# Reading the last 4 rows per partition of the last batch of K by a four-block transfer on four DMA engines

## Chip, cores, metric

The kernel runs on one core of one Trainium2 chip. The metric is device microseconds of one execution, as a median of several executions. Before the change it was 139.41 us (three runs, 139.39 to 139.55).

## The reference, cut to what matters

The program is one decode step of a transformer block for 4 sequences: layer norm, attention over the last 2,048 cached positions (4 key/value heads of 128, 32 query heads), residual, layer norm, gated feed-forward, residual. Everything is bf16.

```python
Hkv, Sk = k_cache.shape[1], k_cache.shape[2]          # 4, 8192
W = min(4096, max(256, Sk // 4))                      # 2048
k = jnp.repeat(k_cache[:, :, Sk - W:, :], rep, axis=1)
scores = jnp.einsum("bhqd,bhkd->bhqk", q, k) * (Dh ** -0.5)
p = _softmax(scores, axis=-1)
...
h2 = h + _B_ref(_layernorm(h, axis=-1), B_w1, B_w3, B_w2)
```

One execution reads 55.6 MB: the query weights, 2 MB of keys and 2 MB of values per sequence, the output weights, and three feed-forward matrices. Each byte is used once.

## The kernel before

All large loads are issued on the SyncE queue (SP), in order, into five buffers of 32 KB per partition. The order is query weights, keys of batches 0 to 3, values of batches 0 to 3, output weights, `w1`, `w3`, `w2`. Keys of one batch go to 128 partitions, 64 rows (16 KB) to each; partition `p` holds block `p // 4` of head `p % 4`.

```python
def load_k(b):
    t = stream.tile([P, SLOT], BF16, tag="s")
    out = []
    for k in range(BS):
        v = t[:, k * JK * Dh : (k + 1) * JK * Dh]
        nc.sync.dma_start(
            out=v,
            in_=A_k_cache[b + k, :, Sk - W : Sk, :].rearrange("g (pp j) d -> pp g (j d)", pp=PK),
        )
        out.append(v)
    return out
# ... (values: four runs of 4 KB to a partition)

def emit_scores(u):
    b, n = units[u]
    kT_v = kT_tiles[u][:].rearrange("d j (pp g) -> d g j pp", g=Hkv)
    for g in range(Hkv):
        nc.tensor.matmul(
            scores_ps[QD * g : QD * (g + 1), n * 512 : (n + 1) * 512],
            lhsT=qz[:, b, g * QD : (g + 1) * QD],
            rhs=kT_v[:, g, :, :], start=(b == 0), stop=(b == B - 1),
        )
# ... (softmax, values, output projection, feed-forward)
# the last load, w2, comes in pieces of 16, 5, 4, 2 and 1 rows per partition
```

## Time and profile before

| | before |
|---|---|
| median time | 139.41 us |
| span of the profiled run | 137.4 us |
| mean rate of the loads | 406 GB/s |
| last of 16 completions of the last load | 133.59 us |

These are the busy times, the rows of the 40 time slices, and the queues, from the page of the kernel before. Each digit of the DMA row is the busy tenth of the 16 DMA engines in a slice; the row below it is what they moved.

```profile
span 137.4 us, 2307 instructions
...
PE 71.2 (52%) x1045; PEld 45.2 (33%) x1045; DVE 36.3 (26%) x63; ACT 29.0 (21%) x28; POOL 1.6 (1%) x7
...
PE   0152304798989889100995579544090530802960
...
DMA  5999999999999999999999999999999999998950
GB/s 155 444 402 520 391 391 444 420 429 444 405 440 392 421 421 414 423 495 476 401 391 424 453 428 397 459 467 401 409 459 439 426 409 430 448 458 359 420 217 2
DMA packets 4773, 55.74 MB, mean 406 GB/s; under 512 B 376, under 2 KB 408, under 8 KB 2716
...
q1 hardware_dynamic: 4724, 55.58, 95.4%
q8 instruction: 8, 0.13, 0.3%
...
q14 instruction: 1, 0.01, 0.0%
```

PE (the matmuls; PEld is the loading of their weights) is busy 52% of the span and no other compute engine more than 26%, and the DMA row is full from the second slice to the end of the loads: the kernel is bound by its stream of loads. The lines q8 and q14 are small. They are DMA packets of the kind that the profile calls "instruction"; the records below show them taking turns with the data packets on the same 16 DMA engines.

The end of the chain of waits of the kernel before (start us, length us, what) says which load that is. The line below it is from the time line.

```profile
95.17 37.81 DMA t<-in_B_w_dram
132.98 0.04 issue
133.02 1.04 PE y_ps L428 x9
134.06 0.02 issue
134.09 0.42 DVE res L438
```

```profile
133.64 0.11 PEld L428 LDWEIGHTS <-hgT 128*32 128x32 bf16 x3 [0.30 <-issue]
```

The matmuls wait for the last piece of the weights but one until 132.98 us. The last piece lands at 133.59 us (below), and the last four matmuls start just after, at about 133.64 us; the chain calls this last gap "issue" and does not name the load. A copy and the store follow.

The second reading needs the engines one by one. The trace has 16 completion writes for each large load and four for each of the small loads of `x`, which have 4 rows (6.50, 6.56, 6.61 and 6.72 us for one of them). They are read here as one by each engine that takes part. The kernel before:

```
load                        its 16 completions, us
keys, batch 3               41.54 to 42.07 (14 engines)   43.27  43.45
values, batch 0             46.51 to 47.02 (14)           48.17  48.19
w1, first half              89.29 to 89.77 (9)   90.63   90.89 to 91.10 (6)
w2, last piece              131.79 to 132.28 (7)   133.00   133.34 to 133.59 (8)
instruction packets         16 KB at 31.70 41.45 52.82 72.20 78.17 83.90 104.06 130.81, 8 KB at 81.93
```

The engines start nearly level (7.52 to 8.16 us for the first large load, 12.42 to 12.91 for the second) and fall apart one by one. The packet records show why. Each 16 KB instruction packet takes 0.88 to 0.96 us and begins where a data packet of one engine ends, and that engine is 1.40 to 1.42 us behind for the rest of the run; no two of the eight fall on the same engine. The single 8 KB packet sets one engine back by 0.84 us. The last of the 16 engines ends the stream of loads, so 7 engines idle for more than a microsecond at the end.

For later comparison, two microseconds of the stretch table of the kernel before (the busy time of each engine in a stretch of the span, with the number of its instructions), in the load of the first values. The last two columns are the DMA engines' busy share and GB/s (a share above 1 is possible, since a packet counts whole in the microsecond in which it starts, and neighbours overlap by a few ns: the 4 KB packets take 159 ns each and follow at about 155).

```profile
core 0: us, PE busy (x) PEld busy (x) DVE busy (x) ACT busy (x) POOL busy (x), PEclk, DMA share, GB/s
...
42.00:43.00 1.00, 1.00 (x21) 1.00 (x20) 0.43 (x1) 0.00 (x0) 0.00 (x0) 1.00 0.97 389
43.00:44.00 1.00, 0.87 (x16) 0.79 (x14) 0.80 (x2) 1.00 (x2) 0.00 (x0) 1.00 1.03 426
```

### The profile page before, as it was taken

The numbers are of one execution on the slowest core, as the hardware profiler recorded it, in microseconds if no ns is written. First come the engines' busy times: TensorE is split into PE (matmuls) and PEld (weight loads), VectorE is DVE, ScalarE is ACT, GpSimd is POOL, SyncE is SP. The second block draws the span as 40 slices with busy tenths as digits, with TensorE's granted clock in tenths as the row PEclk, the third lists the DMA queues.
The fourth block names the chain that finished last, engine by engine and source line by source line (L and its number), as shares of the span: only waits on it lengthen the run. The fifth ranks groups of instructions, "written<-read, shape, count | busy, mean of one in ns | idle before, by whom it ended". The sixth has DMA issues, their size and how long they took to land.

```text
span 137.4 us, 2307 instructions
## 1 busy us (share of the span) xinstructions
PE 71.2 (52%) x1045; PEld 45.2 (33%) x1045; DVE 36.3 (26%) x63; ACT 29.0 (21%) x28; POOL 1.6 (1%) x7
## 2 busy tenths in 40 slices
PE   0152304798989889100995579544090530802960
PEld 0110001175656565000894457221030210302830
DVE  6430000244444444601400300530003970160001
ACT  0400000155564646098610000000005000000000
POOL 4000000000000000000000000000000000000000
PEclk9999999999999999975555555558655586555555
DMA  5999999999999999999999999999999999998950
GB/s 155 444 402 520 391 391 444 420 429 444 405 440 392 421 421 414 423 495 476 401 391 424 453 428 397 459 467 401 409 459 439 426 409 430 448 458 359 420 217 2
DMA packets 4773, 55.74 MB, mean 406 GB/s; under 512 B 376, under 2 KB 408, under 8 KB 2716
## 3 DMA queue, kind: packets, MB, share of 16 engines
q1 hardware_dynamic: 4724, 55.58, 95.4%
q8 instruction: 8, 0.13, 0.3%
q10 hardware_dynamic: 40, 0.02, 0.0%
q14 instruction: 1, 0.01, 0.0%
HBM read 55.59 MB, written 0.01 MB: 405 GB/s over the span
## 4 chain that ended last, share of the span: by engine, by line
DMA 70%; PE 19%; ACT 6%; SPq 1%; DVE 1%; issue 1%; ACTq 0%
DMA t<-in_B_w_dram 54%; DMA t<-in_A_wq_dram 15%; PE kt_ps L270 9%; ACT kT L276 5%; PE scores_ps L255 5%; PE q_ps L222 3%; PE g_ps L398 2%; SPq L97 1%; PE y_ps L428 1%; DVE q_sb L232 1%; ACT q_sb L233 0%; DVE res L438 0%; PE qt_ps L236 0%; ACTq L276 0%
## 5 line engine op out<-in xcount | busy, mean ns | idle before, releaser
L276 ACT COPY kT<-kt_ps 128x1024 bf16<-128x1024 bf16 x16 | 15.8, 1014 | 12.0 <-PE kt_ps L270 12.0
L270 PE MATMUL kt_ps<-ident,t 128*128 128x128 bf16 x256 | 16.5, 219 | 0.0
L270 PEld LDWEIGHTS <-t 128*128 128x128 bf16 x256 | 14.4, 98 | 5.0 <-issue 4.9
L274 DVE COPY kT<-kt_ps 128x1024 bf16<-128x1024 bf16 x16 | 11.1, 692 | 15.2 <-PE kt_ps L270 15.2
L398 PEld LDWEIGHTS <-hnT 128*32 128x32 bf16 x128 | 5.5, 140 | 25.0 <-issue 22.7
L222 PE MATMUL q_ps<-t,xnT 128*4 128x512 bf16 x64 | 7.2, 615 | 12.0 <-DMA t<-in_A_wq_dram 12.0
L398 PE MATMUL u_ps<-t,hnT 128*32 128x448 bf16 x64 | 6.4, 576 | 10.6 <-DMA t<-in_B_w_dram 10.6
L255 PE MATMUL scores_ps<-kT,qz 128*32 128x512 bf16 x64 | 9.9, 609 | 3.1 <-ACT kT L276 3.1
L428 PE MATMUL y_ps<-t,hgT 128*32 128x256 bf16 x112 | 6.7, 415 | 7.6 <-DMA t<-in_B_w_dram 7.6
L398 PE MATMUL g_ps<-t,hnT 128*32 128x448 bf16 x64 | 6.3, 574 | 8.0 <-DMA t<-in_B_w_dram 8.0
L322 PE MATMUL OT_ps<-PT_sb,t 128*128 128x8 bf16 x256 | 7.4, 168 | 1.9 <-issue 1.7
L428 PEld LDWEIGHTS <-hgT 128*32 128x32 bf16 x112 | 4.8, 139 | 10.0 <-issue 5.5
L349 PE MATMUL y_ps<-t,o 128*32 128x256 bf16 x128 | 7.2, 418 | 1.7 <-DMA t<-in_A_wo_dram 0.9
L322 PEld LDWEIGHTS <-t 128*128 128x128 bf16 x256 | 7.3, 104 | 2.1 <-issue 2.0
L222 PEld LDWEIGHTS <-xnT 128*4 128x4 bf16 x64 | 2.0, 111 | 16.4 <-issue 16.1
L308 PE MATMUL pt_ps<-Dm,Pm 128*128 128x128 bf16 x16 | 1.9, 308 | 9.3 <-DVE Dm L301 9.3
L349 PEld LDWEIGHTS <-o 128*32 128x32 bf16 x128 | 5.1, 144 | 3.5 <-issue 1.2
L412 DVE RECIPROCAL eg<-eg 128x896 f32<-128x896 f32 x1 | 5.8, 5754 | 0.0
L232 DVE TENSOR_SCALAR q_sb<-q_ps 128x512 bf16<-128x512 f32 x1 | 0.7, 692 | 17.8 <-PE q_ps L222 17.8
L233 ACT ACTIVATE q_sb<-q_ps 128x512 bf16<-128x512 f32 x1 | 0.6, 597 | 21.4 <-DVE q_sb L232 21.4
L308 PEld LDWEIGHTS <-Pm 128*128 128x128 bf16 x16 | 1.6, 142 | 9.8 <-ACT Pm L294 9.8
L294 ACT ACTIVATE Pm<-scores_ps,nmax 128x2048 bf16<-128x2048 f32 x1 | 4.8, 4783 | 0.0
(67 smaller groups left out, 37.0 us busy)
## 6 DMA issues: line engine op xcount, KB each, us to landing
t<-in_B_w_dram SPq DMA_DIRECT2D x4, 3584.0 KB
t<-in_A_k_cache_dram SPq DMA_DIRECT2D x4, 2048.0 KB, 25.6
t<-in_A_v_cache_dram SPq DMA_DIRECT2D x4, 2048.0 KB, 33.0
t<-in_A_wo_dram SPq DMA_DIRECT2D x2, 4096.0 KB, 32.5
t<-in_A_wq_dram SPq DMA_DIRECT2D x2, 2048.0 KB, 9.6
t<-in_A_wq_dram SPq DMA_DIRECT2D x1, 4096.0 KB, 21.0
t<-in_B_w_dram SPq DMA_DIRECT2D x1, 4096.0 KB, 39.9
t<-in_B_w_dram SPq DMA_DIRECT2D x1, 1280.0 KB, 34.9
```

What stands on the lines that cost most here:

```text
L222: nc.tensor.matmul(q_ps[QD * g : QD * g + B, hf * 512 : (hf + 1) * 512], lhsT=xnT[:, kc, :], rhs=wq_t[:, c0 : c0 + 512], start=(kc == 0), ...
L255: nc.tensor.matmul(scores_ps[QD * g : QD * (g + 1), n * 512 : (n + 1) * 512], lhsT=qz[:, b, g * QD : (g + 1) * QD], rhs=kT_v[:, g, :, :], ...
L270: nc.tensor.transpose(out=kt_ps[:, jj, :], in_=k_v[:, n * NJ + t * TB + jj, :], identity=ident[:])
L274: nc.vector.tensor_copy(out=kT[:, t * TB : (t + 1) * TB, :], in_=kt_ps[:])
L276: nc.scalar.copy(out=kT[:, t * TB : (t + 1) * TB, :], in_=kt_ps[:])
L294: nc.scalar.activation(out=Pm[:].rearrange("q (c jq) -> q jq c", jq=NSB), in_=scores_ps[:].rearrange("q (jq c) -> q jq c", jq=NSB), func=A ...
L308: nc.tensor.matmul(pt_ps[:, jj, :], lhsT=Pm[:, (jb * JPB + jj) * P : (jb * JPB + jj + 1) * P], rhs=Dm[:], start=True, stop=True)
L322: nc.tensor.matmul(OT_ps[:, b, g * REP : (g + 1) * REP], lhsT=v_t[:, g, j, :], rhs=PT_sb[:, j, g * QD + b * REP : g * QD + (b + 1) * REP], ...
L349: nc.tensor.matmul(y_ps[QD * j : QD * (j + 1), :], lhsT=o4[:, i, :, :].rearrange("p b s -> p (b s)"), rhs=loaded["wo"][i][:, j * CG : (j + ...
L398: nc.tensor.matmul(out_ps[QD * j : QD * (j + 1), hf, :HF], lhsT=hnT[:, k, :], rhs=loaded[kind][k][:, c0 : c0 + HF], start=(k == 0), stop=( ...
L412: nc.vector.reciprocal(out=eg[:], in_=eg[:])
L428: nc.tensor.matmul(y2_ps[QD * j : QD * (j + 1), :], lhsT=hgT[:, i, :], rhs=loaded["w2"][i][:, j * CG : (j + 1) * CG], start=False, stop=(i ...
```

## The change

The keys of the last batch come in two transfers. The first takes 60 of 64 rows per partition, as before. The second takes the last 4 rows (1 KB per partition, 128 KB in all) with the head as the outer dimension, so as four blocks of 32 partitions. The intent: the four blocks go to four DMA engines, as the 4-row loads of `x` with their four completions let expect, so twelve engines carry 8 KB less each and four carry 24 KB more. If the four are engines that finish early, the late ones finish earlier. The last group of score matmuls is split to follow the new partition order of these rows.

```diff
+    JT = 4
...
             v = t[:, k * JK * Dh : (k + 1) * JK * Dh]
-            nc.sync.dma_start(
-                out=v,
-                in_=A_k_cache[b + k, :, Sk - W : Sk, :].rearrange("g (pp j) d -> pp g (j d)", pp=PK),
-            )
+            n = (JK - JT) * Dh if b + k == B - 1 else JK * Dh
+            k_v = A_k_cache[b + k, :, Sk - W : Sk, :].rearrange("g (pp j) d -> pp g (j d)", pp=PK)
+            nc.sync.dma_start(out=v[:, :n], in_=k_v[:, :, :n])
+            if n < JK * Dh:
+                nc.sync.dma_start(out=v[:, n:], in_=k_v.rearrange("pp g x -> g pp x")[:, :, n:])
...
+        js = NJ - JT if u == len(units) - 1 else NJ
+        for j0, j1 in ((0, js), (js, NJ)):
+            ...
+            kT_v = kT_tiles[u][:, j0:j1, :].rearrange(
+                "d j (pp g) -> d g j pp" if j0 == 0 else "d j (g pp) -> d g j pp", g=Hkv
+            )
+            # then the four matmuls, on columns n*512 + j0*PK to n*512 + j1*PK
```

More of the change, by code (lines that the diff above doesn't have):

```diff
@@ L42 @@
     KC = D // P
-    FC = F // P
     NK = W // P
     NSB = W // 512
-    assert B == 4 and D == KC * P and F == FC * P and Hq * Dh == 4096
+    assert B == 4 and D == KC * P and F % P == 0 and Hq * Dh == 4096
     assert Dh == P and W == NK * P and B * Hq == P and Hkv == 4
@@ L251, in emit_scores @@
         b, n = units[u]
-        kT_v = kT_tiles[u][:].rearrange("d j (pp g) -> d g j pp", g=Hkv)
-        for g in range(Hkv):
-            z0 = (b * Hkv + g) * QD
-            nc.tensor.matmul(
-                scores_ps[QD * g : QD * (g + 1), n * 512 : (n + 1) * 512],
-                lhsT=qz[:, b, g * QD : (g + 1) * QD],
-                rhs=kT_v[:, g, :, :],
-                start=(b == 0),
-                stop=(b == B - 1),
-            )
+        js = NJ - JT if u == len(units) - 1 else NJ
+        for j0, j1 in ((0, js), (js, NJ)):
+            if j0 == j1:
+                continue
+            kT_v = kT_tiles[u][:, j0:j1, :].rearrange(
+                "d j (pp g) -> d g j pp" if j0 == 0 else "d j (g pp) -> d g j pp", g=Hkv
+            )
+            for g in range(Hkv):
+                nc.tensor.matmul(
+                    scores_ps[QD * g : QD * (g + 1), n * 512 + j0 * PK : n * 512 + j1 * PK],
+                    lhsT=qz[:, b, g * QD : (g + 1) * QD],
+                    rhs=kT_v[:, g, :, :],
+                    start=(b == 0),
+                    stop=(b == B - 1),
+                    skip_group_check=True,
+                )
     nt = 0
```

## The prediction

> What bounds the kernel. The DMA stream. On the profile page the DMA row is 9 tenths or more in 36 of 40 slices at 406 GB/s, PE is busy 52%, DVE 26%, ACT 21%. The chain of waits gives 70% of the span to loads; its last piece is the wait for the feed-forward weights until 132.98 us, then 4 us of matmul, copy and store. So only the DMA engine that finishes last counts.
>
> The DMA packet records and completion times show that the 16 engines do not finish together. Each load's 16 completions start within 0.5 us of each other. After an "instruction" packet of 16 KB (eight in the span, 31.7 to 130.8 us, about 0.93 us each) one engine stays about 1.42 us behind for the rest of the run; one 8 KB instruction packet (81.9 us) costs another 0.84 us. At the end seven engines finish their last weight packet at 131.47 to 131.99 us and nine at 132.70 to 133.18 us. The last one sets the time.
>
> Which engines the change loads. [...] The 4-row loads of x agree in count: four packets at a time. By start times I follow these four engines through: three are early finishers (131.77, 131.80, 131.99), the fourth took the 8 KB instruction packet and ends at 132.70.
>
> Costs. Packet spacing is 80, 155, 305, 607 ns for 2, 4, 8, 16 KB, so about 4.7 ns plus 27.2 bytes per ns; a 15 KB packet is estimated at 569 ns, a 1 KB packet at 42 ns. All engines: 8 packets of 15 KB in place of 16 KB, -0.30 us. The four: 32 packets of 1 KB, +1.36 us, net +1.06 us. One more issue on the SP queue, four more score matmuls (the last group took 0.62 us for four), perhaps +0.25 us of PE near 55 us: off the path, since weights are issued over 25 us before they land.
>
> New finishes (estimate): twelve untouched engines, last 133.18 - 0.30 = 132.88; three of the four 132.83, 132.86, 133.05; the fourth 132.70 + 1.06 = 133.76. If that engine takes the 8 KB packet again, the end moves +0.58 us, to 140.0; if the packet falls elsewhere, about -0.1 us. A further risk is that four engines write into partition ranges that others write at the same time; no record here shows whether that slows either, and it could add 1 us or more. I take 139.9 us, 8 in 10 between 139.1 and 141.3. Chances: faster by over 2% 0.01, within 2% 0.95, slower by over 2% 0.04.
>
> What would show it: in the packet records, 128 packets of 1 KB near 41 to 44 us, four chains of 32, about 42 ns apart (longer: write conflicts). Completions of the last load: four late by about 1.06 us more, twelve 0.30 us earlier. The 8 KB packet still on one of the four. The chain still ends in the weights' DMA. PE, DVE, ACT busy unchanged within 0.5 us.
>
> What would make it wrong: instruction packets moving to other engines (the program has eight more PE instructions and one more issue), 1 KB packets much dearer than estimated, or conflicts at the destination. If none of the four is late, the intended gain, at most 0.30 us, appears.

The count of four rests on the loads of `x`. 132.70 + 1.06 = 133.76 us for the engine that comes last, against 133.18 before, is the +0.58 us, and 139.41 + 0.58 gives the 140.0.

## The result and the profile after

The changed kernel takes 140.33 us (six runs, 140.25 to 140.44) against 139.42 us for the kernel before in the same rounds (139.34 to 139.55). The ratio is 1.0064, with a 95% interval of 1.0051 to 1.0077. A ratio here is always the mean time of one kernel's fast runs over that of the other's fast runs in the same rounds, so it is not quite the ratio of the medians quoted. The change makes the kernel 0.6% slower. The result is correct.

The same lines of the page of the changed kernel:

```profile
span 138.4 us, 2316 instructions
...
PE 69.9 (50%) x1049; PEld 44.7 (32%) x1049; DVE 36.4 (26%) x63; ACT 29.2 (21%) x28; POOL 1.6 (1%) x7
...
PE   0152204799898989500595687136080440801940
...
DMA  5999989999999999999999999999999999899940
GB/s 154 441 414 511 426 388 398 445 426 421 432 402 339 419 419 421 417 462 497 398 426 403 436 439 421 456 423 414 439 456 411 414 439 477 379 432 408 418 186 2
DMA packets 4905, 55.74 MB, mean 403 GB/s; under 512 B 380, under 2 KB 540, under 8 KB 2848
...
q1 hardware_dynamic: 4856, 55.58, 95.3%
q8 instruction: 8, 0.13, 0.3%
...
q14 instruction: 1, 0.01, 0.0%
```

The bytes are the same, there are 132 more packets, and the instruction packets are as many as before. VectorE and ScalarE (DVE, ACT) busy times have not moved; PE went from 71.2 to 69.9 us at a mean granted clock of 0.775 against 0.743. In the row of rates the 13th slice (41.5 to 45.0 us) has 339 GB/s in place of 392.

The end of the chain of waits of the changed kernel:

```profile
96.40 37.66 DMA t<-in_B_w_dram
134.06 0.04 issue
134.10 0.61 PE y_ps L436 x8
134.71 0.03 issue
134.73 0.43 PE y_ps L436 x4
135.16 0.02 issue
135.19 0.42 DVE res L446
```

The weights still end the chain: the wait for the last piece but one ends at 134.06 us in place of 132.98, and the last four matmuls start at 134.73 us, just after the last piece has landed (134.69 us, below).

The completions of the changed kernel:

```
load                        its 16 completions, us
keys, batch 3, 60 rows      41.31 to 41.73 (15 engines)   43.81
keys, batch 3, 4 rows       43.86  43.87  43.90  43.92 (four engines)
values, batch 0             47.01 to 47.45 (10)   48.62 to 48.73 (6)
w1, first half              89.69 to 90.03 (6)    91.20 to 91.41 (9)    92.29
w2, last piece              132.20 to 132.53 (4)   133.68 to 133.93 (11)   134.69
instruction packets         16 KB at 31.77 43.83 54.60 73.74 79.77 86.28 104.38 131.62, 8 KB at 83.59
```

Two things went wrong at once.

First, one engine is alone at the end. It leaves the group at `w1`, where it is 0.88 us behind the next one, right after the 8 KB instruction packet. The packet records tie it to the change: that packet starts where a packet of `w1` ends that had begun just after a completion write at 82.526 us; 34.289 us earlier (the distance of undisturbed completions) the same engine wrote its completion of the first values at 48.237 us. That is one of four writes at 48.230 to 48.269 us, which follow the ends of the four 4-row transfers (42.962 to 43.021 us) in the same order; the two other late ones, 48.336 and 48.348, are the engines of the first two instruction packets. So one of the four engines with 24 KB more is also the one that takes the 8 KB packet. Without it the last completion would be about that of the next one, 133.93.

Second, the other engines are late too. The 60-row transfer of the keys ends 0.23 us earlier at its first completion (41.54 to 41.31), as intended. But from there to the first completion of the values it takes 5.70 us in place of 4.97. The same two microseconds of the stretch table, for the changed kernel:

```profile
42.00:43.00 1.00, 0.40 (x8) 0.15 (x4) 0.14 (x1) 0.89 (x1) 0.00 (x0) 1.00 1.15 289
43.00:44.00 1.00, 1.00 (x13) 0.55 (x13) 0.00 (x0) 0.00 (x0) 0.00 (x0) 1.00 0.97 295
```

The engines are as busy as before and move 289 and 295 GB/s in place of 389 and 426. The packets tell what waits. Value packets of 4 KB take 159 ns in the kernel before; here about 90 of them, of all the other engines, take up to 300 ns between 41.9 and 43.8 us. The 1 KB packets take 46 ns for the first twenty or so of each engine's 32, and then mostly 65 to 88 ns.

### The profile page after: what moved, and what is told of

The parts are those of the page before. It is cut to its first block, busy times and chain, and to the rows that moved or that the text cites. A ratio compares the mean times of both kernels' runs of the same rounds, so it can differ in the third digit from the quotient of the medians.

```text
span 138.4 us, 2316 instructions
## 1 busy us (share of the span) xinstructions
PE 69.9 (50%) x1049; PEld 44.7 (32%) x1049; DVE 36.4 (26%) x63; ACT 29.2 (21%) x28; POOL 1.6 (1%) x7
## 4 chain that ended last, share of the span: by engine, by line
DMA 68%; PE 23%; ACT 4%; SPq 1%; DVE 1%; issue 1%; ACTq 0%
DMA t<-in_B_w_dram 53%; DMA t<-in_A_wq_dram 15%; PE kt_ps L278 11%; PE scores_ps L262 5%; ACT kT L284 4%; PE q_ps L224 3%; PE g_ps L406 2%; SPq L97 1%; PE qt_ps L238 1%; PE y_ps L436 1%; DVE q_sb L234 1%; DVE res L446 0%; ACTq L284 0%
## 5 line engine op out<-in xcount | busy, mean ns | idle before, releaser
L278 PE MATMUL kt_ps<-ident,t 128*128 128x128 bf16 x256 | 18.3, 232 | 0.0
L278 PEld LDWEIGHTS <-t 128*128 128x128 bf16 x256 | 16.0, 105 | 6.1 <-issue 6.1
L262 PE MATMUL scores_ps<-kT,qz 128*32 128x512 bf16 (+2 forms) x68 | 10.5, 581 | 2.8 <-ACT kT L284 2.8
L436 PE MATMUL y_ps<-t,hgT 128*32 128x256 bf16 x112 | 5.7, 368 | 8.6 <-DMA t<-in_B_w_dram 8.6
L330 PEld LDWEIGHTS <-t 128*128 128x128 bf16 x256 | 7.3, 104 | 2.0 <-issue 1.8
L436 PEld LDWEIGHTS <-hgT 128*32 128x32 bf16 x112 | 4.3, 127 | 10.4 <-issue 6.3
L357 PE MATMUL y_ps<-t,o 128*32 128x256 bf16 x128 | 5.1, 337 | 0.8 <-DVE o L346 0.8
L419 DVE TENSOR_SCALAR eg<-eg 128x896 f32<-128x896 f32 x1 | 0.6, 627 | 16.8 <-ACT eg L418 16.8
```

Of the source, the lines that this page charges most:

```text
L262: nc.tensor.matmul(scores_ps[QD * g : QD * (g + 1), n * 512 + j0 * PK : n * 512 + j1 * PK], lhsT=qz[:, b, g * QD : (g + 1) * QD], rhs=kT_v ...
L278: nc.tensor.transpose(out=kt_ps[:, jj, :], in_=k_v[:, n * NJ + t * TB + jj, :], identity=ident[:])
L330: nc.tensor.matmul(OT_ps[:, b, g * REP : (g + 1) * REP], lhsT=v_t[:, g, j, :], rhs=PT_sb[:, j, g * QD + b * REP : g * QD + (b + 1) * REP], ...
L357: nc.tensor.matmul(y_ps[QD * j : QD * (j + 1), :], lhsT=o4[:, i, :, :].rearrange("p b s -> p (b s)"), rhs=loaded["wo"][i][:, j * CG : (j + ...
L436: nc.tensor.matmul(y2_ps[QD * j : QD * (j + 1), :], lhsT=hgT[:, i, :], rhs=loaded["w2"][i][:, j * CG : (j + 1) * CG], start=False, stop=(i ...
```

## The experiments

The coincidence of the 8 KB packet is read from the trace and asks for a test. The slow stretch has rivals. Theory D: four engines write into partitions that other engines are filling, and that slows the writes. Rival S: reading 1 KB at steps of 16 KB is slow at the source. Rival G, which came up after the first four runs: all engines together get through only about 100 packets per microsecond. Twelve kernels were run. "Untouched" engines are those that carry nothing extra. All gave correct results by the comparison.

### split16: the second transfer, but on 16 engines

```diff
-nc.sync.dma_start(out=v[:, n:], in_=k_v.rearrange("pp g x -> g pp x")[:, :, n:])
+nc.sync.dma_start(out=v[:, n:], in_=k_v[:, :, n:])      # and emit_scores as before
```

> The kernel before with the last 4 rows of the last batch of K in their own transfer, but in the old partition order, so on all 16 DMA engines: same 1 KB reads at a 16 KB step, same 128 packets of 1 KB, 8 to an engine. Theory D (packets of four engines collide with the others' writes at the destination): no value packet longer than about 160 ns near 42 to 44 us, all engines +0.04 us, time within 0.1% of before (139.4 us). Rival S (1 KB reads at a 16 KB step are slow at the source): value packets of 200 to 300 ns there as in the changed kernel, every engine about 0.6 us later, time +0.4% or more.

Measured: 139.40 us against 139.54; ratio 0.9992 (0.9978 to 1.0007). No value packet is slowed but the two that follow an instruction packet, as in the kernel before; all 128 packets of 1 KB take 46 ns; the last completion is at 133.61 us. The stretch of split16:

```profile
42.00:43.00 1.00, 1.00 (x22) 1.00 (x19) 0.28 (x1) 0.00 (x0) 0.00 (x0) 1.00 1.00 397
43.00:44.00 1.00, 1.00 (x19) 0.90 (x17) 0.80 (x2) 0.85 (x1) 0.00 (x0) 1.00 0.99 410
```

The rates are those of before. S falls: the same small reads, on 16 engines, cost nothing.

### four_contig: four engines, but 32 KB read in one run

```diff
-in_=k_v.rearrange("pp g x -> g pp x")[:, :, n:]
+in_=A_k_cache[b + k, :, 0 : PK * JT, :].rearrange("g (pp j) d -> g pp (j d)", pp=PK)
```

> The changed kernel with the 4-row transfer reading 32 KB in one run per engine (wrong rows on purpose, so a wrong result) and writing the same places from the same four engines. Theory D: as the changed kernel, value packets up to 300 ns, 140.3 us (+0.6%). Rival S: slow value packets gone, the twelve other engines 0.30 us early instead of 0.35 us late; the end is then set by the engine with the 8 KB instruction packet alone, about 139.9 us (+0.4%).

Measured: 140.27 us; ratio 1.0055 (1.0040 to 1.0070). It reads wrong rows, and the comparison passed within its tolerance all the same, so the comparison does not see 4 of 64 rows in one batch. Value packets take up to 307 ns, and the last completions are 132.10 to 132.63 (4), 133.66 to 133.94 (11), 134.66. The stretch of four_contig:

```profile
42.00:43.00 1.00, 0.41 (x8) 0.17 (x4) 0.00 (x0) 0.68 (x1) 0.00 (x0) 1.00 1.07 254
43.00:44.00 1.00, 1.00 (x17) 0.72 (x14) 0.00 (x1) 0.00 (x0) 0.00 (x0) 1.00 0.96 303
```

As the changed kernel, although the source is read quite differently. S falls a second time.

### add_spread and add_own: an added, useless load, spread or not

Both keep all loads of the kernel before and add a useless 32 KB for each of four engines, into a scratch tile. To make room there are two buffers of transposed keys in place of three. In add_spread:

```diff
+k_g = A_k_cache[b + k, :, Sk - W : Sk, :].rearrange("g (pp j) d -> g pp (j d)", pp=PK)
+nc.sync.dma_start(out=scr[:, : 4 * Dh], in_=k_g[:, :, (JK - 4) * Dh :])
```

> The kernel before with all its loads, plus a useless copy of the four-engine transfer into a scratch tile, spread over all 128 partitions as in the changed kernel (control for the next one; two transposed-K buffers in place of three make room). Theory D and S alike: value packets up to 300 ns near 42 to 44 us, untouched engines about 0.65 us later than before, the last engine 1.36 + 0.8 us later, time about +1.1% (141.0 us).

Measured: 142.68 us; ratio 1.0205 (1.0167 to 1.0242), nearly twice the extra that was expected (2.05% against 1.1%). Value packets take up to 240 ns, less than in the changed kernel, but the 1 KB packets take up to 409 ns and go on until 46.6 us. Untouched engines are about 0.65 us late at the values (first completion 47.17 against 46.51), as expected; the loaded ones end at 135.08 to 137.17 us. The direction was right, the size not.

In add_own the added bytes go only to partitions 0 to 15: block `i` of the four writes partitions `4i` to `4i+3`. No run shows which engine fills which partition; the runs compare places only.

```diff
+for h in range(4):
+    nc.sync.dma_start(
+        out=scr[h : h + 13 : 4, :].rearrange("p (t x) -> p t x", t=8),
+        in_=k_g[:, h * 8 : (h + 1) * 8, (JK - 4) * Dh :],
+    )
```

> As add_spread, same source reads and same count of 1 KB packets per engine, but engine i writes only partitions 4i to 4i+3[...]. Theory D: no value packet longer than about 165 ns, untouched engines end as before (0.0 us), the four 1.36 us later, so the one with the 8 KB instruction packet ends near 134.06 us: time +0.6% (140.3 us). Rival S: as add_spread, slow value packets, +1.1%.

Measured: 141.80 us; ratio 1.0172 (1.0135 to 1.0208). Half of the expectation held. Three value packets above those of the kernel before pass 175 ns (the longest of the three 214), the first completion of the values is at 46.43 us, and the untouched engines' last completions are those of before. But the four themselves are later than expected: from the third of their four transfers on the packets slow down, to as much as 493 ns, and they end at 134.74 to 135.81 us. Why is open. The records carry no engine numbers, so whether these are the engines' own partitions is not shown. What is shown is the place: the values are not slowed here (first completion 46.43 us, 46.51 before), and are in add_other below (47.53).

### add_other: the same, into partitions 16 to 31

```diff
-        out=scr[h : h + 13 : 4, :].rearrange("p (t x) -> p t x", t=8),
+        out=scr[16 + h : 29 + h : 4, :].rearrange("p (t x) -> p t x", t=8),
```

> As add_own, but the four engines write only partitions 16 to 31[...]. Theory D (collisions at the destination): [...] Rival G (a common limit of about 100 packets a us for all engines together, seen in the earlier runs as 92 to 98 a us in the slow stretch): no particular four engines slow; as add_own, only the 1 KB packets themselves slow down.

Measured: 141.47 us, the median of three runs; ratio 1.0145 (1.0126 to 1.0165); a fourth run, of 148.53 us, counts as slow and is left out. Theory D's expectation was value packets over 200 ns for one to two us on some of the other engines, and none on the rest. Neither expectation held. All untouched engines were slowed, not some: their value packets took 305 to 331 ns for a microsecond, about double, and their first completion of the values is at 47.53 us, 1.02 us later than before. So the place matters (compare add_own), but the harm is not confined to some of the engines.

### add_big: the same bytes in 4 KB packets, to every fourth partition

```diff
+nc.sync.dma_start(out=scr[0:P:4, : 16 * Dh], in_=k_g[:, PK - 8 :, (JK - 16) * Dh :])
```

> As add_spread, same 32 KB for each of the four engines[...], but in 8 packets of 4 KB, each to one partition. Theory D: the other engines' value packets slow as in add_spread (untouched engines 0.3 us or more later). Rival G: packets stay below the limit, no value packet over 165 ns, untouched engines as before, the four +1.24 us: the one with the 8 KB instruction packet ends near 133.94 us, time about +0.5% (140.2 us).

Measured: 140.57 us; ratio 1.0075 (1.0059 to 1.0091). Value packets take up to 245 ns (one 269), and the first completion of the values is at 47.01 us, 0.5 us late. The collision does not need small packets. This speaks for D and against G.

### v_1k: small packets on all engines, no added transfer

```diff
+VQ = 4 if b + k == 0 else 1      # values of batch 0 in four passes of 4 rows: runs of 1 KB
+v = t[...].rearrange("p (q g j d) -> p q g j d", q=VQ, g=Hkv, d=Dh)
...
-lhsT=v_t[:, g, j, :],
+lhsT=v_t[:, j // v_t.shape[3], g, j % v_t.shape[3], :],
```

> The kernel before with the values of batch 0 read in packets of 1 KB[...] (2,048 packets at 380 a us if each takes 42 ns). Theory D: no collision, the load takes 5.4 us in place of 5.0, all later loads +0.47 us, time +0.3% (139.9 us). Rival G: 2,048 packets at about 100 a us take about 20 us, time +10%.

Measured: 139.94 us; ratio 1.0030 (1.0014 to 1.0047), the number that D gave. 2,048 packets of 1 KB take 46 ns nearly throughout, which is about 380 per microsecond. G falls.

### jt2: 2 rows in place of 4

```diff
-    JT = 4
+    JT = 2
```

> The changed kernel with 2 rows in place of 4 (16 packets of 1 KB... each of 0.5 KB, 32 to an engine, 16 KB in all): half the bytes moved to the four engines. If the extra delay goes with the bytes (D), untouched engines end about 0.15 us later than before and the engine with the 8 KB instruction packet near 133.9 us in landing (0.3 us after the last landing of before): +0.2% (139.7 us). Under G, which counts packets, as many packets as in the changed kernel: untouched engines about 0.6 - 0.15 us later than without collisions, +0.3 to +0.5%.

Measured: 139.57 us; ratio 1.0020 (0.9992 to 1.0048), six runs from 139.20 to 140.64. (The packets are of 0.5 KB.) Neither expectation held: there was next to no collision. Value packets take 159 ns but for a handful (up to 189), and all 0.5 KB packets take 27 ns. The last completions are 131.87 to 132.13 (4), 132.64 to 133.45 (11) and 133.76. The latest of the eleven is 0.14 us earlier than the 133.59 us of before, as intended; the one with the 8 KB packet takes it back. So the collision does not simply go with the bytes.

### own_big4, own_big2, other_big4: the 8 KB packet, and the place

These are as add_own, but in 8 packets of 4 KB per engine, so that the slow small packets of add_own are out of the way: on four engines, on two, and on four engines into partitions 16 to 31.

```diff
+for h in range(4):
+    nc.sync.dma_start(
+        out=scr[h : h + 13 : 4, :].rearrange("p (t x) -> p t x", t=2),          # own_big4
+        in_=k_g[:4, PK - 8 + 2 * h : PK - 6 + 2 * h, (JK - 16) * Dh :],
+    )
# own_big2:   out=scr[h : h + 5 : 4, :], in_=k_g[:2, ...]
# other_big4: out=scr[16 + h : 29 + h : 4, :]
```

> The kernel before plus a useless 32 KB for each of four engines, in 8 packets of 4 KB, written only to partitions 0 to 15 (where 1 KB packets left the other engines alone). Expected: no slow value packet, eleven other engines land the last weights as before (latest 133.6 us), the four +1.24 us: three land near 133.3 to 133.6, the one with the 8 KB instruction packet near 134.25 us, alone at the end. Time +0.5% (140.1 us). If the 8 KB packet were not what matters, the last landing would stay near 133.6 us and the time at 139.5 us.

> As own_big4 for two engines only. [...] last landing near 134.25 us, +0.5%. [...] the two loaded engines land near 133.3 to 133.6 us, the one with the 8 KB packet at 133.0 us, and the time is that of before within 0.1%: then the same added load costs nothing on engines without that packet.

(The first outcome is for the case that the engine of the 8 KB packet is one of the two loaded, the second for the case that it is not.)

> As own_big4, but written to partitions 16 to 31[...]. If the place written decides: all other engines' value packets slow, untouched engines 0.5 to 1.0 us later in all landings after it, time at least +0.5% more than own_big4 (141 us). If only small packets collide: as own_big4.

Measured, with the completions of the last piece of `w2`:

```
            median us  ratio (95%)               last completions, us
own_big4    139.80     1.0025 (1.0010 to 1.0040)   131.73 to 132.16 (4)   133.11 to 133.64 (11)   134.26
own_big2    139.35     0.9997 (0.9980 to 1.0013)   131.69 to 132.18 (5)   133.01   133.18 to 133.56 (10)
other_big4  140.97     1.0121 (1.0095 to 1.0147)   133.59 to 133.90 (4)   134.93 to 135.26 (11)   136.03
```

(One run of other_big4, 147.69 us, counts as slow and is left out, of the median too.) In own_big4 one engine is alone at the end, at 134.26 us where 134.25 was expected. The time grew by 0.34 us, less than the 0.67 us of that completion: in the profiled runs the span grew by 0.24 us. The steps after the last completion were quicker: 0.39 us to the copy of the output against 0.50 before, 0.59 us for issuing the store against 0.70, and a shorter end of the program after that. In own_big2 two engines carry the same 32 KB more: of the seven early completions of before (131.79 to 132.28) five are left, and the late group has ten in place of eight. The engine of the 8 KB packet ends at 133.01 us as in the kernel before (133.00), so it is not one of the two, and the time is that of before. So the same added load per engine is free on two early engines and costs 0.25% as soon as two more carry it, one of which takes the 8 KB packet.

The stretch of own_big4, then that of other_big4. They differ only in which 16 partitions of an unused tile are written.

```profile
42.00:43.00 1.00, 1.00 (x22) 1.00 (x20) 0.62 (x1) 0.18 (x1) 0.00 (x0) 1.00 0.96 381
43.00:44.00 1.00, 0.81 (x17) 0.70 (x14) 0.76 (x2) 1.00 (x2) 0.00 (x0) 1.00 1.07 442
```

```profile
42.00:43.00 1.00, 0.41 (x8) 0.19 (x4) 0.00 (x0) 0.70 (x1) 0.00 (x0) 1.00 1.09 225
43.00:44.00 1.00, 1.00 (x17) 0.70 (x14) 0.00 (x0) 0.00 (x0) 0.00 (x0) 1.00 0.91 205
```

381 and 442 GB/s against 225 and 205. Rank by rank, every completion of the values and of the last piece is at least 1.2 us later in other_big4. The place written decides; small packets are not needed for it. Not all of the 1.6 to 1.9 us at the end is lost in these two microseconds: the profiled run of other_big4 is the slowest of its three fast ones, and from 46 to 54 us, after the added transfers had landed, its value packets still took about 174 ns, against 159 in own_big4. Why is not known.

### two_blocks: the one version left to try

```diff
-    JT = 4
+    JT = 2
...
-nc.sync.dma_start(out=v[:, n:], in_=k_v.rearrange("pp g x -> g pp x")[:, :, n:])
+for c in range(0, Hkv, 2):
+    nc.sync.dma_start(
+        out=v[c * PK : (c + 2) * PK, n:], in_=k_v.rearrange("pp g x -> g pp x")[c : c + 2, :, n:]
+    )
```

> The only version that the runs so far point to: 2 rows in place of 4, read by two transfers of two blocks each[...] (64 packets of 0.5 KB each), which do not take the 8 KB instruction packet. Without collisions: fourteen engines 0.15 us earlier (latest landing 133.45 us), the two about 1.35 us later (near 133.4 us), the engine of the 8 KB packet at 132.85 us; time 139.3 us, 0.1% under before, which is at the edge of what 5 rounds can show. With collisions as in the changed kernel: all untouched engines 0.3 us or more later, time +0.2% or more.

(Which engines carry two blocks is cut; the expectation took them for the two of own_big2, which do not take the 8 KB packet. No run shows that they are the same.)

Measured: 140.09 us against 139.43; ratio 1.0055 (1.0027 to 1.0083), six runs from 139.50 to 141.06. It was meant to avoid the engine of the 8 KB packet, and it loses: 42 value packets, besides the four that follow an instruction packet, took over 175 ns, the longest 1,095 ns, and completions end at 134.35 us. No version beat the kernel before; own_big2 only ties with it, and moves nothing useful.

## Why the prediction came out as it did

The prediction was 139.9 us (139.1 to 141.3), within 2%. Measured were 140.33 us. The direction and the main mechanism held; one term of the sum had the wrong sign. The sum gave +0.58 us for the end of the loads; the range held because it left room for a collision that the sum did not contain.

- "The DMA stream ... only the DMA engine that finishes last counts": held. The chain still ends in the weights' load, and DVE and ACT did not move. (The wait until 132.98 us that the prediction quotes is for the last piece but one.) PE moved by 1.3 us, more than the stated 0.5 us; the mean granted clock differed too.
- "Three are early finishers, the fourth took the 8 KB instruction packet": held. In the changed kernel one of the four loaded engines takes it again. own_big4 and own_big2 show by experiment that the added load is free on two of the engines, and that on four exactly one engine comes out last, at the time worked out beforehand.
- "Packet spacing ... 4.7 ns plus 27.2 bytes per ns": held where nothing collides. The 15 KB packets took 573 ns, the first 1 KB packets of the change came 42 ns apart, and v_1k came out as worked out.
- "Twelve untouched engines, last 133.18 - 0.30 = 132.88": this is the step that failed. Their last packet ended at 133.63 us, 0.75 us later than predicted (this engine is told from the loaded ones by its place in the order of completions). They won the 0.30 us at the keys and lost more in the 2 us after, to the writes of the four. The engine with the 8 KB packet was predicted at 133.76 us and ended at 134.37, later by 0.61 us, in the same stretch.
- "A further risk is that four engines write into partition ranges that others write at the same time": that is the missing term. The prediction named it, put no amount into the middle value for it, and had no record to size it from. four_contig, split16 and v_1k exclude the source and the packet count; own_big4 against other_big4 shows that the place decides (ratios 1.0025 and 1.0121).
- "If none of the four is late, the intended gain ... appears": would not have held. Without the 8 KB packet the last completion would, by the reckoning above, still have been at about 133.93 us, 0.34 us after that of before. No run shows this kernel without it.

In completions of the profiled runs, the last one moved from 133.59 to 134.69 us, by 1.10 us. Of this 0.34 us is what the collision leaves after the intended gain, and 0.76 us the engine that stands alone. The profiled run of the changed kernel was the slowest of its six; the medians differ by 0.91 us.

Open: why all untouched engines are slowed when the added bytes go to 16 partitions only (add_other, value packets of 305 to 331 ns), why the 1 KB packets themselves are slow in partitions 0 to 15, where the values are not slowed (add_own, up to 493 ns), and why 64 KB in two blocks at a time collided (two_blocks) and in four did not (jt2). Only one pair of places was compared with all else the same (partitions 0 to 15 and 16 to 31), and no run writes the second place while nothing else is written there; which engine fills which partition is not shown, and that the writes of two engines to the same partitions must coincide is argued, not shown.

## What to carry to other kernels

When a kernel is bound by its loads, look at the completions of each DMA engine and not only at the mean rate: here the last engine set the end of the kernel, and instruction packets made engines late one by one, by 0.84 to 1.42 us each. Before giving early engines more bytes, check that they are early for good, that is, that no later packet falls on them (own_big2 was free, ratio 0.9997; own_big4, with the engine of the 8 KB packet, had 1.0025), and try more than one place for the bytes (1.0025 in partitions 0 to 15, 1.0121 in partitions 16 to 31, other_big4). In this kernel the four blocks, written to all 128 partitions while the other engines went on with the loads, cost the whole stream more than they relieved it (the last completion but one came 0.34 us later where up to 0.30 us earlier was intended); in one run, jt2, there was next to no such cost.
